# Eight of twelve fp32 recalls become three f32r products each, in an attention-with-memory plus gated feed-forward kernel

## The chip, the cores and the metric

The kernel runs on one core of a Trainium2 chip. The metric is the device time of one execution in microseconds (us); the time before is the median of three runs. Engines are TensorE (PE; PEld is its weight loading), VectorE (DVE), ScalarE (ACT), GpSimd (POOL) and SyncE (SP), which here only issues transfers. Each takes its own instructions in order and waits on semaphores for the others.

## The reference

A layer norm of x (2048 tokens of 448) feeds two branches whose results are added to x: attention with a memory over four blocks of 512 tokens and 16 heads of 28, and a gated feed-forward layer of width 1792. The part that matters, cut down:

```python
for s in range(N):                       # 4 blocks of 512 tokens
    ...
    p = softmax(logits, axis=-1)
    a_dot = jnp.einsum("bhqk,bhkd->bhqd", p, vs)
    pq = phi(qs)
    num = jnp.einsum("bhld,bhde->bhle", pq, M)
    den = jnp.einsum("bhld,bhd->bhl", pq, z)[..., None] + 1e-6
    o = g * (num / den) + (1.0 - g) * a_dot
    outs.append(o)
    M = M + jnp.einsum("bhld,bhle->bhde", phi(ks), vs)
    z = z + jnp.einsum("bhld->bhd", phi(ks))
```

A recall is `num` and `den` of four heads of one block: the memory M, with z as a further column, is multiplied by phi of the queries. Block 0 has an empty memory, so there are three blocks with four groups of heads each: twelve recalls.

## The kernel before

The work has a front, in which TensorE, ScalarE and VectorE follow the order of the program text, and a main part, in which the feed-forward products, the softmax attention and the output projection are interleaved. In the front GpSimd's and SyncE's queues are ordered by a scheduler when the program is built; they are not in the set `FRONT` of engines whose order is the text's.

The front goes block by block (L504, `b` from 0 to 3; "block 2" is the pass with `b` = 2). A pass first makes the values of its four token tiles: `values(b, t)` (L343) multiplies eleven pairs of high and low parts into one PSUM bank, and `store_values` (L338) copies the bank out on ScalarE. Large products throughout are made this way: a float32 operand is split into a high part of type f32r (a copy on ScalarE) and the rest (a subtraction), and three products, high by high, high by low and low by high, are summed in PSUM.

Then come seven strips of keys and queries, `keys_queries(b, c)` (L350), eleven products over 512 columns each, followed by ScalarE and VectorE work on the bank. Strips with queries also store phi of the queries to `fd[b]` (L368). The memory's update (L379) follows the strips; `mst` has two sets of four tiles of 112 x 128 (four heads of 28 rows), written in turn by even and odd blocks.

Recalls lag by one block: pass `b` = 2 recalls block 1 and pass 3 recalls block 2, four each; block 3's own four are made at the end of pass 3. In passes 2 and 3, `phi_queries` (L392) loads four phi tiles of 112 x 512 from DRAM, in buffers of the tag "e". The recall of group t - 1 stands behind `values(b, t)` for t = 1, 2, 3; the fourth stands behind the first `keys_queries`. `recall` (L397) is one fp32 product, which the profile shows as two passes of TensorE, into a bank of tag "m" or "pd"; then on VectorE a transpose (L402), `weigh` (an addition L132, a reciprocal L133, a weighting L136) and a second transpose (L404); then a transfer to `od` (L405) that GpSimd issues. In pass 2, VectorE also makes the statistics of the next block's rows, and ScalarE their root (L301), behind the first `values`.

Two shared sets of buffers are used by the change: tag "4k" (four buffers, L149; `qk` of `keys_queries`, later `hh`) and tag "2k" (two, L152; early weights, later `sg`). A `qk` buffer is free again when its transfer to `qd` (L363) has landed.

Of the kernel before, what the change touches and what calls it, by code (L numbers as in the profile page):

```python
# [9 lines left out]
F32 = mybir.dt.float32  # L10
F32R = mybir.dt.float32r
AF = mybir.ActivationFunctionType
# [4 lines left out]
P = 128  # L17
# [11 lines left out]
GW = HG * DH  # L29
# [32 lines left out]
def kernel(  # L62
# [11 lines left out]
    V, A, G, T = nc.vector, nc.scalar, nc.gpsimd, nc.tensor  # L74
# [33 lines left out]
    def x_block(b):  # L108
        return x[b * L:(b + 1) * L, :].rearrange("(t p) d -> p t d", p=P)
# [5 lines left out]
    def bank(name, tag):  # L115
        return ps.tile([P, L], F32, name=name, tag=tag, bufs=banks[tag])
# [10 lines left out]
    def weigh(pool, num, g, add):  # L127

        r = pool.tile([P, 16], F32, name="rc", bufs=2)
        n3 = num.rearrange("p (m c) -> p m c", c=32)  # L130
        if add:
            V.tensor_scalar_add(r, n3[:, :, DH], add)  # L132
            V.reciprocal(r, r)  # L133
        else:
            V.reciprocal(r, n3[:, :, DH])
        V.scalar_tensor_tensor(n3[:, :, :DH], n3[:, :, :DH], g, r.unsqueeze(2).to_broadcast([P, 16, DH]),  # L136
                               op0=ALU.mult, op1=ALU.mult)
# [6 lines left out]
    mid = ctx.enter_context(tc.tile_pool(name="mid", bufs=3, reuse_waits="tile"))  # L144
# [4 lines left out]
    def four_k(dtype, name):  # L149
        return mid.tile([P, 2, L], dtype, name=name, tag="4k", bufs=4)  # L150
# [125 lines left out]
    with tc.tile_pool(name="front", bufs=2) as sb, tc.manual_schedule(engines=FRONT):  # L276
# [7 lines left out]
        mst = [[sb.tile([GW, P], F32, name=f"mst{n}_{i}", bufs=1) for i in range(NG)] for n in range(2)]  # L284
# [3 lines left out]
        def statistics(b, t0, steps):  # L288

            stats = sb.tile([P, steps, 6], F32, name=f"stats{steps}")  # L290
            mv = sb.tile([P, steps, 2], F32, name=f"mv{steps}")
            vh = sb.tile([P, steps], F32, name=f"vh{steps}")
            for t in range(steps):
                V.bn_stats(stats[:, t, :], acc[b][:, t0 + t, :])
                V.bn_aggr(mv[:, t, :], stats[:, t, :])
            V.tensor_scalar(vh, mv[:, :, 1], EPS, -0.5, op0=ALU.add, op1=ALU.mult)
            return mv, vh

        def root(vh):
            y = sb.tile([P, vh.shape[1]], F32, name=f"y{vh.shape[1]}")  # L300
            A.activation(y, vh, AF.Sqrt, scale=-2.0)  # L301
            return y

        def rstd(mv, vh, y):

            steps = vh.shape[1]
            tm = sb.tile([P, steps], F32, name=f"tm{steps}")
            V.reciprocal(y, y)
            if steps == 1:
                V.tensor_scalar(tm, y, y, vh, op0=ALU.mult, op1=ALU.mult)  # L310
                V.tensor_scalar(y, tm, 1.5, y, op0=ALU.add, op1=ALU.mult)
            else:
                V.tensor_mul(tm, y, y)
                V.tensor_mul(tm, tm, vh)
                V.scalar_tensor_tensor(y, tm, 1.5, y, op0=ALU.add, op1=ALU.mult)
            return [(mv[:, t, 0:1], y[:, t:t + 1]) for t in range(steps)]

        def normalise(b, t, mean, y):
            xn = sb.tile([P, 512], F32, name="xn")
            V.tensor_scalar(xn[:, :D].rearrange("p (m h c) -> p h m c", h=H, c=4),  # L320
                              acc[b][:, t, :].rearrange("p (h m c) -> p h m c", h=H, c=4), mean, y,
                              op0=ALU.subtract, op1=ALU.mult)
            if b == 0:
                A.activation(xn[:, D:], xn[:, 384:D], AF.Copy)
            else:
                G.tensor_copy(xn[:, D:], xn[:, 384:D])
            return xn

        def turn(b, t, xn):
            transpose_split(bank("pt", "s"), xn, xs[b], t)  # L330
# [12 lines left out]
        def values(b, t):  # L343
            pv = bank("pv", "p")
            value_terms(b, t, pv, EARLY[1] if b == 0 else TERMS)
            store_values(b, t, pv)
# [45 lines left out]
        def phi_queries(b, i):  # L392
            phi = sb.tile([GW, L], F32, name="phi", tag="e", bufs=5)
            nc.sync.dma_start(phi, fd[b][i * GW:(i + 1) * GW])
            return phi

        def recall(b, i, phi):  # L397
            ts = sb.tile([P, L], F32, name="ts", bufs=1)
            tb = sb.tile([P, L], F32, name="tb", bufs=2)
            n2 = bank("n2", ("m", "pd")[i % 2])  # L400
            T.matmul(n2, mst[b % 2][i], phi, start=True, stop=True)  # L401
            V.transpose(ts, n2)  # L402
            weigh(sb, ts, gate[:, i:i + 1], MEM_EPS)
            V.transpose(tb, ts)  # L404
            nc.gpsimd.dma_start(od[b][P * i:P * (i + 1)], tb)  # L405
# [28 lines left out]
        def split_qk(c):  # L434
            r = raw_qk[c].rearrange("p (c n) -> p c n", c=4)
            A.activation(wqk[c][:, 0:4, :], r, AF.Copy)
            G.tensor_sub(wqk[c][:, 4:8, :], r, wqk[c][:, 0:4, :].bitcast(F32))
# [66 lines left out]
        for b in range(NB):  # L504
            last = b == NB - 1
            phi, xn = {}, {}
            if b > 1:
                phi = {i: phi_queries(b - 1, i) for i in range(NG)}
            st = None
            for t in range(3 if b == 0 else 0, NT):  # L510
                values(b, t)
                if b > 1 and t > 0:
                    recall(b - 1, t - 1, phi[t - 1])
                if b == 0:
                    split_qk(t)
                if last:
                    continue
                if t == (3 if b == 0 else 0):
                    mv, vh = statistics(b + 1, 0, NT)
                if t == (3 if b == 0 else 0):  # L520
                    st = mv, vh, root(vh)
                if t == (3 if b == 0 else 2):
                    A.activation(one, ident[:, 0:1], AF.Exp)
            if st and b > 0:
                st = rstd(*st)
                for n in range(2):
                    xn[n] = normalise(b + 1, n, *st[n])
            e = {}
            for k, c in enumerate((3, 4, 5, 6, 0, 1, 2) if last else range(7)):
                e[c] = keys_queries(b, c)  # L530
                if b == 0 and c + 4 < 7:
                    split_qk(c + 4)
                if k == 0:
                    if b > 1:
                        recall(b - 1, NG - 1, phi[NG - 1])
                    if b == 0:
                        st = rstd(*st)
                    if b == 0:
                        A.activation(gate, gate, AF.Exp, scale=-1.0)
                        V.tensor_scalar_add(gate, gate, 1.0)  # L540
                        V.reciprocal(gate, gate)
                        V.tensor_scalar(gate_n, gate, -1.0, 1.0, op0=ALU.mult, op1=ALU.add)
                if (b, k) in ((0, 3), (1, 0)):
                    with tc.issue_after(stored[b, c]):
                        nc.sync.dma_start(acc[b + 2], x_block(b + 2))
                if (b, k) in ((2, 1), (3, 0)):
                    with tc.issue_after(stored[b, c]):
                        next(ffn)
                if last:
                    if k > 0:  # L550
                        next(ffn)
                    if 2 <= k < 6:
                        phi[k - 2] = phi_queries(b, k - 2)
                    if k > 4:
                        begin[k - 5]()
                        recall(b, k - 5, phi[k - 5])
                    continue
                if 2 <= k < 6:
                    key_rows(k - 2, e[k - 2])
                if 4 <= k:  # L560
                    update(b, k - 4)
                if k == 6:
                    update(b, 3)
                n = k - 1 if b == 0 else k + 1
                if 2 <= n < 6:
                    turn(b + 1, n - 2, xn[n - 2])
                if 0 <= n < 4 and n not in xn:
                    xn[n] = normalise(b + 1, n, *st[n])
                if b == 2 and k == 6:
                    next(ffn)  # L570
            if last:
                for i in range(2):
                    for _ in range(FILLS[i]):
                        next(ffn)
                    if i == 0:
                        begin[2]()
                    recall(b, i + 2, phi[i + 2])
# [256 lines left out]
```

## Time and profile before

| | us |
|---|---|
| median of 3 runs (lowest, highest) | 689.46 (689.41, 689.59) |
| the profiled execution | 689.46 |
| its span, first to last instruction | 687.7 |
| TensorE, 77.80 to 95.20 us (17.40) | 17.40 busy |
| VectorE, same stretch | 15.40 busy |
| ScalarE, same stretch | 7.06 busy |
| GpSimd, same stretch | 2.48 busy |

A row of instructions reads: line, engine, operation, written and read tiles, shapes and count, then the busy time of all, the mean of one in ns, and the idle time of the engine ahead of them. A row of the timeline reads: start, length, engine, line, operation. The chain of waits follows the program back from its last instruction, at each step to what ended the wait.

### The profile page before, as it was taken

How to read it: one execution, taken by the hardware profiler on the slowest of the kernel's cores; microseconds unless marked ns; L12 is line 12 of the kernel's file. 1: busy time of each engine (PE TensorE's matmuls, PEld its weight loads, DVE VectorE, ACT ScalarE, POOL GpSimd, SP SyncE). 2: the span in 40 equal slices, each digit the busy share in tenths (PEclk: the TensorE clock that was granted, in tenths of full speed). 3: DMA queues.
4: the chain of work that ended last, by engine and by line, in shares of the span. 5: the costliest groups of instructions: out<-in, count | busy, mean ns of one | idle time of the engine just before them, and what ended most of it. 6: DMA issues, size and time to landing. Idle time of an engine off the chain costs nothing.

```text
span 687.7 us, 10438 instructions
## 1 busy us (share of the span) xinstructions
PE 681.7 (99%) x3594; PEld 566.6 (82%) x3594; DVE 567.4 (83%) x994; ACT 342.6 (50%) x563; POOL 151.3 (22%) x349
## 2 busy tenths in 40 slices
PE   8999999999999999999999999999999999999997
PEld 7898888778878787787878878787787878878897
DVE  6765795767788988998898989989898899889863
ACT  4837555343554555543655446454653565446320
POOL 3500020101223222232332222322322322222000
PEclk9999999999999999999999999999999999999999
DMA  7446556696233323243223252314333332423342
GB/s 267 181 150 238 198 214 242 249 330 174 71 94 92 80 86 86 56 128 112 56 64 107 57 141 56 109 47 116 82 94 77 96 71 64 95 79 95 95 153 106
DMA packets 45796, 84.37 MB, mean 123 GB/s; under 512 B 6320, under 2 KB 20400, under 8 KB 45232
## 3 DMA queue, kind: packets, MB, share of 16 engines
q1 hardware_dynamic: 42736, 76.37, 35.8%
q0 software_dynamic: 3008, 7.34, 4.9%
q8 instruction: 28, 0.46, 0.3%
q14 instruction: 24, 0.20, 0.1%
HBM read 51.05 MB, written 32.64 MB: 122 GB/s over the span
## 4 chain that ended last, share of the span: by engine, by line
PE 70%; DVE 14%; issue 9%; POOL 4%; DMA 1%; ACT 1%; SPq 0%; POOLq 0%; ACTq 0%
PE pgu L247 26%; PE pd L173 13%; PE pp L355 10%; PE po L771 5%; PE pv L335 5%; PE st L612 3%; PE pa L687 3%; DVE mx L629 3%; DVE w L666 2%; POOL w L627 2%; DVE acc L174 2%; PE pmm L383 2%; PE n L401 2%; DVE hh L259 1%; DVE mx L633 1%
## 5 line engine op out<-in xcount | busy, mean ns | idle before, releaser
L247 PE MATMUL pgu<-xs,wgu 128*128 128x512 f32 x1232 | 304.1, 394 | 0.0
L247 PEld LDWEIGHTS pgu<-xs,wgu 128*128 128x128 f32 x1232 | 228.2, 188 | 47.4 <-issue 2.2
L173 PE MATMUL pd<-wdn,hh 128*128 128x448 f32 x672 | 156.0, 367 | 0.0
L627 POOL TENSOR_SCALAR_AFFINE_SELECT w<-w 128x256 f32<-128x256 f32 (+1 forms) x160 | 81.2, 509 | 236.4 <-ACT w L616 183.6
L173 PEld LDWEIGHTS pd<-wdn,hh 128*128 128x128 f32 x672 | 122.5, 188 | 12.3 <-issue 0.6
L667 ACT ACTIVATE w<-w 128x1024 f32<-128x1024 f32 (+1 forms) x96 | 87.3, 915 | 65.0 <-DVE w L666 64.2
L666 DVE TENSOR_TENSOR w<-w,mb 128x1024 f32<-128x1024 f32 (+1 forms) x96 | 98.9, 1045 | 0.1
L616 ACT ACTIVATE w<-st 128x512 f32<-128x512 f32 x128 | 74.9, 590 | 45.3 <-PE st L612 44.9
L629 DVE TRANSPOSE_TENSOR_REDUCE mx<-w 128x32 f32<-128x1024 f32 x64 | 79.0, 1235 | 17.0 <-POOL w L627 17.0
L355 PE MATMUL pp<-xs,wqk 128*128 128x512 f32 x308 | 77.7, 401 | 0.0
L174 DVE TENSOR_TENSOR acc<-pd,acc 128x448 f32<-128x448 f32 x112 | 67.1, 599 | 1.2 <-PE pd L173 1.1
L355 PEld LDWEIGHTS pp<-xs,wqk 128*128 128x128 f32 x308 | 56.8, 188 | 13.4 <-issue 2.4
L258 ACT ACTIVATE hh<-sg 128x512 fp32r<-128x512 f32 x56 | 35.2, 628 | 56.4 <-DVE sg L256 49.3
L612 PE MATMUL st<-qk 84*128 84x128 f32 (+3 forms) x256 | 61.9, 312 | 0.0
L255 ACT ACTIVATE sg<-pgu 128x512 f32<-128x512 f32 x56 | 33.2, 594 | 49.4 <-PE pgu L247 49.2
L612 PEld LDWEIGHTS st<-qk 84*128 84x128 f32 x256 | 47.6, 189 | 6.9 <-ACT w L616 0.3
L656 DVE STREAM_TRANSPOSE mb<-top 128x1024 f32<-128x1024 f32 x32 | 39.8, 1242 | 10.5 <-POOL top L653 10.1
L362 DVE TENSOR_TENSOR qk<-pp,qk 128x512 fp32r<-128x512 f32 x28 | 19.3, 688 | 29.8 <-ACT e L360 23.7
L259 DVE SCALAR_TENSOR_TENSOR hh<-sg,hh 128x512 fp32r<-128x512 f32 x56 | 38.7, 691 | 2.6 <-ACT hh L258 2.4
L335 PE MATMUL pv<-wv,xs 128*128 128x448 f32 x176 | 39.6, 376 | 0.4 <-DVE xs L102 0.3
L687 PE MATMUL pa<-w,vv 128*32 128x128 f32 (+3 forms) x512 | 39.7, 436 | 0.2
L256 DVE SCALAR_TENSOR_TENSOR sg<-sg,pgu 128x512 f32<-128x512 f32 x56 | 37.3, 665 | 1.8 <-PE pgu L247 1.6
(100 smaller groups left out, 640.6 us busy)
## 6 DMA issues: line engine op xcount, KB each, us to landing
qk<-qd SPq DMA_DIRECT2D x192, 112.0 KB
qd<-qk SPq DMA_DIRECT2D x28, 512.0 KB
raw<-in_w_ffn SPq DMA_DIRECT2D x14, 512.0 KB
vd<-vst SPq DMA_DIRECT2D x4, 1024.0 KB
vv<-vd SPq DMA_DIRECT2D x16, 256.0 KB
od<-w POOLq DMA_DIRECT2D x16, 256.0 KB, 3.8
sums<-od SPq DMA_DIRECT2D x32, 128.0 KB
out<-acc SPq DMA_DIRECT2D x16, 224.0 KB
```

The source lines that it names most:

```text
L173: T.matmul(pd[:, :D], l, r, start=n == 0, stop=n == len(mms) - 1)
L174: V.tensor_add(acc[b][:, t, :], pd[:, :D], acc[b][:, t, :])
L247: T.matmul(dst, wgu[f][:, w, side * P:(side + 1) * P], xs[b][:, a, :], start=n == 0, stop=n == len(TERMS) - 1)
L335: T.matmul(pv[:, :D], xs[b][:, a, t * P:(t + 1) * P], wv[w], start=n == 0, stop=n == len(TERMS) - 1)
L355: T.matmul(pp, wqk[c][:, w, :], xs[b][:, a, :], start=n == 0, stop=n == len(TERMS) - 1)
L612: T.matmul(st[:, at:at + L - kb * P], self.qk[:KS, 1, h, kb * P:(kb + 1) * P], self.qk[:KS, 0, h, kb * P:], start=True, stop=True)
L616: A.activation(w, st, AF.Copy)
L627: G.affine_select(d, d, pattern=pattern, base=0, channel_multiplier=-1, compare_op=ALU.is_ge, fill=MASK)
L629: V.tensor_reduce(mx[:, 16 * (n - 1):16 * (n + 1)], w3[:, n // 2, :2 * L].rearrange("p (b n) -> p b n", n=32), axis=mybir.AxisListType.X, ...
L666: V.tensor_sub(w, w, m)
L667: A.activation(w, w, AF.Exp, scale=SCALE)
L687: T.matmul(pa[32 * j:32 * j + 32, kb * P:], self.vv[:, kb, 32 * j:32 * j + 32], self.pairs[j // 2].block(j % 2, kb), start=kb == 0, stop=k ...
```

## The change

Passes 2 and 3 call a new function `parts` behind each `values`, after the recall that stands there. It makes the high and low parts of a phi tile in a buffer of tag "4k" and those of the memory's tile in one of tag "2k", two copies on ScalarE and two subtractions on GpSimd, and returns three pairs of operands. `recall` then multiplies the three pairs into its bank. The four recalls of block 3 pass a plain tile and stay one fp32 product.

```diff
+        def parts(b, i, phi):
+
+            f = four_k(F32R, "phis")[:GW]
+            m = mid.tile([P, 4, P], F32R, name="ms", tag="2k", bufs=2)[:GW]
+            A.activation(f[:, 0, :], phi, AF.Copy)
+            G.tensor_sub(f[:, 1, :], phi, f[:, 0, :].bitcast(F32))
+            A.activation(m[:, 0, :], mst[b % 2][i], AF.Copy)
+            G.tensor_sub(m[:, 1, :], mst[b % 2][i], m[:, 0, :].bitcast(F32))
+            return [(m[:, a, :], f[:, w, :]) for a, w in ((0, 0), (0, 1), (1, 0))]
+
         def recall(b, i, phi):
...
             n2 = bank("n2", ("m", "pd")[i % 2])
-            T.matmul(n2, mst[b % 2][i], phi, start=True, stop=True)
+            terms = phi if isinstance(phi, list) else [(mst[b % 2][i], phi)]
+            for n, (l, r) in enumerate(terms):
+                T.matmul(n2, l, r, start=n == 0, stop=n == len(terms) - 1)
...
                 values(b, t)
-                if b > 1 and t > 0:
-                    recall(b - 1, t - 1, phi[t - 1])
+                if b > 1:
+                    if t > 0:
+                        recall(b - 1, t - 1, phi[t - 1])
+                    phi[t] = parts(b - 1, t, phi[t])
```

## The prediction

> **What bounds the kernel now.** I read the page's head first, then the chain of waits in order of time over the two stretches that the change touches.
>
> ```profile
> span 687.7 us, 10438 instructions
> PE 681.7 (99%) x3594; PEld 566.6 (82%) x3594; DVE 567.4 (83%) x994; ACT 342.6 (50%) x563; POOL 151.3 (22%) x349
> ```
>
> ```profile
> 78.06 4.42 PE pv L335 x22
> 82.48 0.86 PE n L401 x2
> 83.34 2.21 PE pv L335 x11
> 85.55 0.86 PE n L401 x2
> 86.41 2.21 PE pv L335 x11
> 88.61 0.86 PE n L401 x2
> 89.47 2.51 PE pp L355 x11
> 91.99 0.86 PE n L401 x2
> ...
> 115.00 4.42 PE pv L335 x22
> 119.42 0.86 PE n L401 x2
> ...
> 128.93 0.86 PE n L401 x2
> ```
>
> Columns: start, length, what (us). Each piece starts where the last one ended: in both stretches TensorE sets the time and waits for nothing. A recall is two passes, 0.86 us; the eleven products of `values` take 2.21, those of `keys_queries` 2.51. So what shortens a recall shortens the run, and what makes TensorE wait here lengthens it. The profiled run took 689.46 us, the median of the runs: span 687.7, 1.76 around it.
>
> **The change part by part.**
>
> *The products.* Three products over 512 columns, at the pace of the `keys_queries` group (2.51 / 11 = 0.228), take 0.685 in place of 0.86: 0.175 saved each, 1.4 us over eight, if nothing waits.
>
> *The splitting.* `parts(t)` puts two copies on ScalarE behind the store of `values(t)` and two subtractions on GpSimd. The nearest rows:
>
> ```profile
> L436 ACT ACTIVATE wqk<-stage 128x512 fp32r<-128x512 f32 x4 | 2.4, 621 | 0.0
> L377 ACT ACTIVATE kn<-pk 128x256 f32<-128x256 f32 x3 | 1.1, 370 | 0.0
> L324 ACT ACTIVATE xn<-xn 128x64 f32<-128x64 f32 x4 | 1.0, 254 | 3.8 <-DVE xn L320 3.8
> L437 POOL TENSOR_TENSOR wqk<-stage,wqk 128x512 fp32r<-128x512 f32 x4 | 5.1, 1293 | 4.8 <-ACT wqk L436 4.8
> L432 POOL TENSOR_TENSOR wv<-wv_raw,wv 128x448 fp32r<-128x448 f32 x4 | 4.6, 1167 | 5.9 <-ACT wv L431 5.9
> L326 POOL COPY xn<-xn 128x64 f32<-128x64 f32 x12 | 3.1, 262 | 38.3 <-DVE xn L320 24.6 <-PE pt L95 13.6
> L355 PE MATMUL pp<-xs,wqk 128*128 128x512 f32 x308 | 77.7, 401 | 0.0
> L355 PEld LDWEIGHTS pp<-xs,wqk 128*128 128x128 f32 x308 | 56.8, 188 | 13.4 <-issue 2.4
> ```
>
> The phi copy is L436's: 0.62. The memory's (128 columns) lies between 0.25 and 0.37; I take 0.29, and it ends under the first subtraction. Phi's subtraction is L437's: 1.29. The memory's subtraction has no row: between 0.26 (the 64-column copy) and 1.17 (448 columns); the line through L432 and L437, 1.97 ns a column, gives 0.54, which I take. Only the last recall's operands differ in partitions (112 for 128); I take no gain for that. The third product needs the memory's low part, so it comes last.
>
> *When the parts are ready, block 2.* The timeline of before:
>
> ```profile
> 80.31 0.55 ACT L339 ACTIVATE vst<-pv 128x448 f32<-128x448 f32 x1 [2.21 <-PE pv L335]
> 83.16 0.53 ACT L339 ACTIVATE vst<-pv 128x448 f32<-128x448 f32 x1
> 83.38 0.72 DVE L402 STREAM_TRANSPOSE ts<-n 128x512 f32<-128x512 f32 x1 [0.36 <-PE n L401]
> 84.63 0.68 DVE L136 SCALAR_TENSOR_TENSOR ts<-ts,gate,rc 128x448 f32<-128x448 f32 x1
> 86.38 0.76 POOL L405 DMA_DIRECT2D od<-tb  x1 [20.41 <-DVE tb L404]
> 89.44 0.56 POOL L405 DMA_DIRECT2D od<-tb  x1 [2.31 <-DVE tb L404]
> ...
> 117.25 0.55 ACT L339 ACTIVATE vst<-pv 128x448 f32<-128x448 f32 x1 [1.26 <-PE pv L335]
> ```
>
> Values 0 end at 78.06 + 2.21 = 80.27. ScalarE stores to 80.86 and copies to 81.48; GpSimd subtracts to 82.79 and 83.33 (an estimated 0.02 to start). TensorE is there at 82.48 and would want the third operand at 82.94. It waits, then loads weights (0.19) and multiplies (0.40), with 0.05 to wake (ScalarE took 0.04 from 80.27): recall 0 ends at 83.97, not 83.34: **+0.63**. Behind the waiting product stand values 2 and all that follows on TensorE.
>
> Recall 1: values 2 end at 86.18. ScalarE's store (83.16, held by the statistics as before) ends at 83.69, the copy at 84.31, the subtractions at 85.62 and 86.16: in time. It ends at 86.87, +0.46 against before. Recall 2: GpSimd also issues the store of recall 0, 3.00 us after `ts` starts (83.38 to 86.38), now at 87.01, until 87.77. Phi's copy is done at 87.39, so the store goes first and the subtractions end at 89.06 and 89.60. Values 3 end at 89.08; the third product waits and ends at 90.24 against 89.47: +0.77. If the subtractions go ahead of the store, it is 89.77, 0.47 less. Recall 3 has the 2.51 of `keys_queries` before it, so its parts (92.28) are in time: +0.59, or +0.12 with the other order. **Block 2 costs 0.59.**
>
> *Block 3* has no statistics; the store of values 0 stands at 117.25 here too, 0.04 after they end. So recall 0 ends at 120.91 against 120.28, +0.63. Recall 1 is in time, +0.46. Recall 2: store of recall 0 at 123.95 to 124.49, subtractions to 126.32, values 3 at 126.02: a wait of 0.25, +0.55. Recall 3 +0.37. **Block 3 costs 0.37.**
>
> *What else hides.* Phi must be in SBUF when ScalarE copies it, earlier than TensorE wanted it:
>
> ```profile
> 75.51 0.46 SPq L394 DMA_DIRECT2D phi<-fd  x1
> 78.19 0.33 SPq L363 DMA_DIRECT2D qd<-qk  x1
> ...
> 79.26 3.27 SPq L394 DMA_DIRECT2D phi<-fd  x3
> ```
>
> ```profile
> od<-tb POOLq DMA_DIRECT2D x3, 256.0 KB, 3.0
> ```
>
> By the landing time of a store of like size (3.0), the four are there by 78.5, 82.3 and, the last two, 85.5 at the latest; copies start at 80.86, 83.69, 86.77 and 89.7. If that cover is gone, the lateness goes to the recall one for one. No DMA is added. The new tiles share buffers with the `qk` stores, the last issued at 78.19, 11 us before the fourth part, and with `sg`, which comes after all eight. The chain starts before each phase of the remaining kernel, so nothing returns the 0.96.
>
> Sum: 0.59 + 0.37 = 0.96 on the profiled 689.46: **690.4 us**. With the subtractions ahead of the store and 0.26 for the small one, only the first recall of each block waits (0.28 less), and the sum is -0.35: 689.1. With 1.17, the first and third recalls' waits grow by 0.63 and, through the store issue, once more: 2.0 and 1.6 at the blocks' ends where 0.59 and 0.37 stood, about 693.0.
>
> **The rivals.**
>
> *The lock, slower.* Two inputs from SBUF on VectorE and a subtraction on GpSimd seem to exclude each other here:
>
> ```profile
> 25.55 1.30 POOL L437 TENSOR_TENSOR wqk<-wqk_raw,wqk 128x512 fp32r<-128x512 f32 x1 [2.81 <-ACT wqk L436]
> 25.80 1.08 DVE L313 TENSOR_TENSOR tm<-y 128x4 f32<-128x4 f32 x1
> 26.91 0.16 DVE L314 TENSOR_TENSOR tm<-tm,vh 128x4 f32<-128x4 f32 x1
> ```
>
> A four-column operation took 1.08 and ended with GpSimd's; its sister took 0.16. In the recall, L136 (0.68, two tiles) wants to start 1.25 after `ts` does (83.38 to 84.63), at 85.26, during a subtraction. If GpSimd's large and small subtraction go back to back it costs nothing; from the point where L136 slips in between, the small one is 0.69 late: block 2's recall 1 then waits to 87.49, recall 2 to 90.98, 0.74 more, and recall 2 of block 3 to 127.65, 0.69 more. 691.8 us. The Trainium skill ("SBUF — State Buffer", "Who interferes with whom") states this: whichever of the two starts first holds a shared port for its whole instruction, the other blocks. The row agrees that VectorE blocked; that GpSimd would then block behind L136 no row of these blocks shows.
>
> *A store issue ahead of a subtraction, slower.* GpSimd takes its queue in order. If the store of recall 0 stood ahead of recall 1's small subtraction, that one would end at 87.77 + 0.54 = 88.31 and recall 1 at 88.95, 2.1 late; later recalls take back 0.5. Two blocks: 3.2 more, 693.6. In program order, ahead of both subtractions every time, each of six recalls would wait about 3 us for the previous one's transposes, store issue and subtractions: +18, 708 us. Against it:
>
> ```profile
> 0.95 0.20 POOL L496 MEMSET heads<- 128x128 f32 x1
> ...
> 1.42 0.31 POOL L427 MEMSET vst<- 128x256 f32 x1
> ```
>
> L496 is written after L427, yet ran before: GpSimd's order follows what is ready, and the subtractions of recall 1 are ready at 84.31, 2.7 before the store. TensorE's clock never fell in the run of before:
>
> ```profile
> core 0: 687.7 us, clock 0.999
> ```
>
> The Trainium skill ("TensorE: Matmul & The Clock Gate", Part 1) says that it halves after some 3.4 us without work; waits of 3 us lie at that edge, and by that page the 708 would be some 5 to 10 us more, an estimate that no run here shows.
>
> *The whole gain, faster.* If no product waits: 689.46 - 1.4 = 688.06. Even 0.26 for the small subtraction leaves the first recall 0.1 late (83.05 against 82.94), so all GpSimd work would have to be quicker than its rows.
>
> *The change doesn't do what it says.* With 112 rows and new weights each time, three products might take 0.86 like the two passes (0.287 each). Then the 1.4 is lost beside the waits, some of which shrink: about 691.3.
>
> **How the numbers follow.** A measurement of this kernel tells about 0.2% (1.4 us) from no change: bounds 688.1 and 690.8. Forecast 0.55 (its own range 689.1 to 690.9, a tenth of it above 690.8), lock 0.17, store ahead 0.08 and program order 0.04, whole gain 0.10 (half below 688.1), no gain 0.06. Slower: 0.06 + 0.17 + 0.08 + 0.04 + 0.06 = 0.41. Faster: 0.05, and 0.03 for a reordered rest of the kernel. Same: 0.51. The range runs from the whole gain, 688.0, past the lock and the dear small subtraction to 693.0; store ahead, program order and half of what lies below are left out.
>
> **What would show it.** Right: recall groups of three products; the first of blocks 2 and 3 some 1.4 to 1.5 us long on the chain with a wait put down to GpSimd's subtraction of the memory; the second and fourth about 0.69. The blocks end 0.6 and about 1 us late on TensorE. Wrong: products far from 0.228, GpSimd's subtractions away from 1.29 and 0.54, VectorE's L136 well over 0.69 beside them, or an `od` issue between the two subtractions of one recall.

## The result, and the profile after

The changed kernel takes 695.37 us (median of 5 runs, 694.86 to 696.47) against 689.46 before: the ratio is 1.0089, with a 95% interval of 1.0078 to 1.0101. It is 5.9 us slower. The forecast was 690.4 with a range up to 693.0, so even the range missed it. The profiled run took the median, 695.37, with a span of 693.6 against 687.7.

The head of the page of the changed kernel: span, then for each engine busy time, share and instructions.

```profile
span 693.6 us, 10502 instructions
...
PE 683.1 (98%) x3602; PEld 567.1 (82%) x3602; DVE 573.4 (83%) x994; ACT 348.3 (50%) x579; POOL 165.7 (24%) x365
```

TensorE's busy time hardly moved (681.7 before), though eight more of its instructions stand there. VectorE has the same 994 instructions and is busy 6.0 us longer: something holds it. Where TensorE lost its time is in the chain of waits of the changed kernel, the same stretch that the prediction shows of the kernel before (start, length, what):

```profile
81.44 1.29 POOL phis L402
...
82.78 0.92 PE n L413 x2
...
83.73 0.73 DVE ts L414
...
84.48 1.30 DVE rc L132
...
86.09 0.69 DVE ts L136
...
86.81 0.72 DVE tb L416
...
87.83 0.06 POOL od L417
...
88.60 0.49 POOL ms L404
...
89.13 0.50 PE n L413
...
98.27 0.85 PE pt L95 x4
...
118.36 4.43 PE pv L335 x22
...
131.90 1.31 POOL phis L402
...
133.25 0.90 PE n L413 x2
134.15 2.06 PE pp L355 x9
```

Lines have moved: the recall's product is now L413, its transposes L414 and L416, its store L417, the subtractions L402 (phi) and L404 (memory). Recall 0 of block 2 ends at 83.70, 0.36 later than before (83.34). Then the chain leaves TensorE altogether. It runs through the whole back half of recall 0 on VectorE (transpose, L132, L136, transpose), through GpSimd's issue of that recall's store, and only then through GpSimd's small subtraction for recall 1. Recall 1 ends at 89.63 instead of 86.41, **3.22 us late**. Its own inputs had nothing to do with recall 0.

The timeline of the changed kernel at that place (start, length, engine, line, operation, idle time before it) shows both halves of it:

```profile
84.44 1.30 POOL L402 TENSOR_TENSOR phis<-phi,phis 112x512 fp32r<-112x512 f32 x1 [1.30 <-ACT phis L401]
84.48 1.29 DVE L132 TENSOR_SCALAR rc<-ts 128x16 f32<-128x16 f32 x1
...
87.83 0.75 POOL L417 DMA_DIRECT2D od<-tb  x1 [2.10 <-DVE tb L416]
88.60 0.48 POOL L404 TENSOR_TENSOR ms<-mst,ms 112x128 fp32r<-112x128 f32 x1
...
89.13 0.50 PE L413 MATMUL n<-phis,ms 112*128 112x512 f32 x1 [2.75 <-POOL ms L404]
```

First, GpSimd's order: phi's subtraction of recall 1 (84.44), **store of recall 0 (87.83), memory's subtraction of recall 1 (88.60)**. GpSimd has nothing to do from 85.74 to 87.83, but the store at the head of its queue waits for VectorE, and the small subtraction waits behind it. Second, VectorE's addition L132, sixteen elements of one input, takes 1.29 us where it takes 0.17 to 0.18 in the kernel before, and ends as GpSimd's subtraction does. It puts the store 1.1 us later still.

The groups of instructions of the changed kernel from 78 to 136 us (both blocks; busy time, mean ns, idle time ahead and its cause):

```profile
L402 POOL TENSOR_TENSOR phis<-phi,phis 112x512 fp32r<-112x512 f32 x8 | 10.4, 1297 | 31.2 <-ACT phis L401 31.1
L413 PE MATMUL n<-phis,ms 112*128 112x512 f32 x24 | 8.8, 434 | 3.2 <-POOL ms L404 2.7 <-POOL phis L402 0.3
L132 DVE TENSOR_SCALAR rc<-ts 128x16 f32<-128x16 f32 x7 | 6.8, 977 | 0.2
...
L404 POOL TENSOR_TENSOR ms<-mst,ms 112x128 fp32r<-112x128 f32 x8 | 3.7, 464 | 0.0
```

L132's mean is 977 ns. The subtractions themselves cost what was forecast, 1297 and 464 ns.

Followed by its landmarks on the chain, the loss of 5.9 us comes in three portions. Block 3's first values start at 118.36 instead of 115.00: **3.36 in block 2**. Most of it is recall 1; 0.41 come later in the block, at the transposes of block 3's normalised rows (L95, 0.85 where the kernel before takes 0.44), whose last piece GpSimd copies (L326, until 98.93) once VectorE has made it (L320). Block 3's recalls end at 134.15 instead of 129.79: **1.00 more in block 3**. A later landmark, the first full group of 32 attention products (`pa`, L701), starts at 209.11 instead of 203.19, and the offset stays the same from there on: **1.56 between the two**, outside the changed code.

### The profile page after: what moved, and what is told of

It reads as the page before. It is cut to its first block, busy times and chain, and to the rows that moved or that the text cites. A ratio compares the mean times of both kernels' runs of the same rounds, so it can differ in the third digit from the quotient of the medians.

```text
span 693.6 us, 10502 instructions
## 1 busy us (share of the span) xinstructions
PE 683.1 (98%) x3602; PEld 567.1 (82%) x3602; DVE 573.4 (83%) x994; ACT 348.3 (50%) x579; POOL 165.7 (24%) x365
## 4 chain that ended last, share of the span: by engine, by line
PE 67%; DVE 15%; issue 10%; POOL 5%; DMA 1%; ACT 1%; POOLq 0%; SPq 0%; ACTq 0%; DVEq 0%
PE pgu L247 25%; PE pd L173 13%; PE pp L355 9%; PE po L785 5%; PE pa L701 4%; PE st L626 3%; PE pv L335 3%; DVE mx L643 2%; POOL w L641 2%; DVE w L680 2%; PE pmm L383 2%; DVE acc L174 1%; DVE hh L259 1%; DVE mx L647 1%; DMA raw<-in_w_ffn 1%
## 5 line engine op out<-in xcount | busy, mean ns | idle before, releaser
L355 PE MATMUL pp<-xs,wqk 128*128 128x512 f32 x308 | 76.2, 396 | 0.0
L701 PE MATMUL pa<-w,vv 128*32 128x128 f32 (+3 forms) x512 | 39.7, 436 | 0.1
L335 PE MATMUL pv<-wv,xs 128*128 128x448 f32 x176 | 38.0, 367 | 0.4 <-POOL wv L444 0.2
```

The lines of the kernel that those rows point to most:

```text
L335: T.matmul(pv[:, :D], xs[b][:, a, t * P:(t + 1) * P], wv[w], start=n == 0, stop=n == len(TERMS) - 1)
L355: T.matmul(pp, wqk[c][:, w, :], xs[b][:, a, :], start=n == 0, stop=n == len(TERMS) - 1)
L701: T.matmul(pa[32 * j:32 * j + 32, kb * P:], self.vv[:, kb, 32 * j:32 * j + 32], self.pairs[j // 2].block(j % 2, kb), start=kb == 0, stop=k ...
```

## The experiments

The theory drawn from this profile had two parts. (a) The store stands ahead of the small subtraction on GpSimd in block 2. (b) GpSimd's subtraction holds VectorE's L132, which makes every store late, and the next subtractions stand behind the store. The main rival was that the lock alone, or GpSimd's load alone, is the cause. Every ratio is to the kernel before, run on the same chip. Three kernels, called "no addition", leave out the addition of 1e-6 in all twelve recalls.

### The store behind the small subtraction

```diff
-                    if t > 0:
-                        recall(b - 1, t - 1, phi[t - 1])
-                    phi[t] = parts(b - 1, t, phi[t])
+                    phi[t] = parts(b - 1, t, phi[t])
+                    if t > 0:
+                        recall(b - 1, t - 1, phi[t - 1])
```

In the recalls of both blocks, the only instruction on GpSimd whose place changes is the store of recall 0 in block 2.

> The one difference from the changed kernel: in block 2 GpSimd's issue of recall 0's store stands behind the small subtraction of recall 1 instead of ahead of it. Theory (the store's place in GpSimd's queue is the 3.2 us of block 2): recall 1 of block 2 ends near 86.8 us instead of 89.6, the third recall then waits for the store issue that stands ahead of its subtractions and gives back about 1 us, so the block gains 1.5 to 2 us; block 3 is as before; 691.9 to 693.9 us, the lower end if the late weight load after block 3 goes too. Rival (the subtractions are late because VectorE and GpSimd lock each other, wherever the store stands): recall 1 still ends after 88.5 us and the time stays at 695 us.

Measured: 693.96 us (692.80 to 694.43), ratio 1.0060 [1.0048, 1.0072]. The timeline of this kernel in block 2:

```profile
84.38 1.30 POOL L402 TENSOR_TENSOR phis<-phi,phis 112x512 fp32r<-112x512 f32 x1 [1.30 <-ACT phis L401]
84.43 1.29 DVE L132 TENSOR_SCALAR rc<-ts 128x16 f32<-128x16 f32 x1
85.64 0.46 POOL L404 TENSOR_TENSOR ms<-mst,ms 112x128 fp32r<-112x128 f32 x1
85.69 0.96 PE L413 MATMUL n<-phis,ms 112*128 112x512 f32 x3
...
87.78 0.75 POOL L417 DMA_DIRECT2D od<-tb  x1 [1.69 <-DVE tb L416]
88.32 1.56 DVE L132 TENSOR_SCALAR rc<-ts 128x16 f32<-128x16 f32 x1
88.55 1.29 POOL L402 TENSOR_TENSOR phis<-phi,phis 112x512 fp32r<-112x512 f32 x1
...
89.89 0.90 PE L413 MATMUL n<-phis,ms 112*128 112x512 f32 x2 [0.79 <-POOL phis L402]
```

Recall 1 now ends at 86.65, in time, where it ended at 89.63: the store's place costs recall 1 its 3 us, and (a) is shown. But the total comes down by only 1.4. Phi's subtraction of recall 2 stands behind the late store (87.78) and starts at 88.55; where no store is ahead of it, it starts at 87.17 (the kernel with the stores on SyncE, below). So TensorE waits at recall 2, and at recall 3 in the same way. Block 3's values start at 117.45: 2.45 of the 3.36 are still there. The stores are as late as before, because L132 is held as before (1.29, 1.56). The chain of this kernel runs, in block 2, through VectorE alone: three held additions, then the normalised rows of block 3 (L320, until 97.33), for which TensorE's transposes (L95, 97.37) wait. TensorE's own products end at 97.32, so both roads are equally late there.

### No addition, in the program's own order, and with the store behind

```diff
-            weigh(sb, ts, gate[:, i:i + 1], MEM_EPS)
+            weigh(sb, ts, gate[:, i:i + 1], 0.0)
```

L132 is gone; the reciprocal (now L135) reads the sums directly.

> The changed kernel, with the addition of 1e-6 ahead of the recalls' reciprocal left out; GpSimd's queue is in the same order. Theory (the addition, a VectorE operation of 0.18 us, was held 1.1 us by GpSimd's subtraction, and the store that GpSimd must issue before its next subtraction was late by that): recall 1 of block 2 ends 1.0 to 1.5 us earlier than in the changed kernel, at 88.1 to 88.6 us, and recall 3 of block 3 waits at most 0.2 us; 692.8 to 694.3 us. Rival (the reciprocal or the weighting is held in the addition's place): recall 1 ends after 89.0 us and the time stays within 0.5 us of 695.4. Second rival (the place of the store alone, at the price first worked out): 693.6 us with no change from the addition.

Measured: 693.53 (692.27 to 693.64), ratio 1.0054 [1.0041, 1.0067]. Its timeline in block 2:

```profile
84.39 1.30 POOL L402 TENSOR_TENSOR phis<-phi,phis 112x512 fp32r<-112x512 f32 x1 [1.30 <-DMA phi<-fd]
84.44 0.26 DVE L135 RECIPROCAL rc<-ts 128x16 f32<-128x16 f32 x1
84.73 1.44 DVE L136 SCALAR_TENSOR_TENSOR ts<-ts,gate,rc 128x448 f32<-128x448 f32 x1
...
87.23 0.75 POOL L417 DMA_DIRECT2D od<-tb  x1 [1.54 <-DVE tb L416]
```

The lock moves to the next instruction: the reciprocal passes beside the subtraction in its 0.26, and the weighting takes 1.44 in place of 0.69. The store comes 0.60 earlier (87.23 for 87.83) and recall 1 ends 0.60 earlier, at 89.03. So the store's time does follow from the lock. That another instruction is held in the addition's place, and that recall 1 ends after 89.0, was the rival's forecast; its time (695) was not met.

Both edits together:

> Both at once: GpSimd's store of recall 0 behind the small subtraction of recall 1, and the addition of 1e-6 left out of the recalls. Theory (the place of the store and the holding of VectorE together make all but the first recalls' waits, which are worth some 0.4 us a block): recall 1 of block 2 ends near 86.7 us, block 3 starts 0.5 to 1.5 us late against the kernel before, block 3 adds less than 0.6, nothing is lost after it; 690.0 to 691.3 us. Rival (a third cause in the changed kernel that neither edit touches): 692 us or more, and the chain names it.

Measured: 690.74 us (690.63 to 691.44), ratio 1.0020 [1.0011, 1.0028]. Over the median before, the loss is 5.9 as changed, 4.5 with the store moved, 4.1 without the addition, and 1.3 with both. By these medians neither edit alone takes away much more than a quarter, both together more than three quarters. How much each is worth by itself can't be read from this exactly: the profiled run without the addition also paid some 1.6 us to a slower TensorE clock (its `values` behind the wait took 3.79 in place of 2.21), of which more below. The one of its four runs whose mean clock was 1.000 took 692.27, a loss of 2.8, about half of the 5.9. With both edits, the profiled run (691.44, the slowest of eleven) starts block 3's values 1.35 late (116.35), of which 0.28 was there ahead of block 2 (78.34 for 78.06).

### GpSimd without stores

```diff
-            nc.gpsimd.dma_start(od[b][P * i:P * (i + 1)], tb)
+            nc.sync.dma_start(od[b][P * i:P * (i + 1)], tb)
```

Made once in the changed kernel and once, as a control, in the kernel before.

> The changed kernel with the recalls' stores issued by SyncE, so nothing on GpSimd waits for a recall. Theory: only the first recall of each block still waits (about 0.4 us late at its end), every later one takes 0.69 us instead of 0.86, and blocks 2 and 3 end within 0.3 us of the kernel before; 688.8 to 690.2 us. VectorE's addition behind a subtraction may still take 1.3 us, and costs nothing. Rival (GpSimd's subtractions are too slow by themselves or by the lock): other recalls wait too, 691.5 us or more. Second rival (SyncE's queue is now held by the stores): TensorE waits for transfers, 692 us or more.

> Control: the kernel before with the recalls' stores issued by SyncE. Theory: GpSimd has nothing to wait for in this stretch anyway and TensorE never stands still, 689.2 to 689.8 us, the same as before. Rival (SyncE's queue is held by the stores): slower by more than 1 us.

Measured: 702.31, ratio 1.0183 [1.0170, 1.0196], and the control 701.08, ratio 1.0169 [1.0156, 1.0182]. Both theories were wrong on the time, and the rival with SyncE's queue was right. As a way out this fails, and the control says that it has nothing to do with the change: SyncE's queue is held by the stores, and transfers for the attention come late (the control's chain has a piece of 3.49 us on the transfer `qk` from `qd`, at 168.20). But the front of the changed kernel is what the experiment was for. From its chain:

```profile
82.85 0.92 PE n L413 x2
...
85.99 0.78 PE n L413 x3
...
92.23 0.69 PE n L413 x3
...
119.81 0.92 PE n L413 x2
...
129.11 0.69 PE n L413 x3
129.80 2.51 PE pp L355 x11
```

Only the first recall of each block waits; the other six take 0.69 to 0.78, and block 3 ends at 129.80 against 129.79 before. In this very run L132 was held for 1.27 beside the subtraction of 84.51. The later additions met less of a subtraction here (0.47 and 0.40 in block 2). So in this run, beyond the first recall of a block, neither the lock nor GpSimd's load of some 14 us costs TensorE anything: here it is the stores in GpSimd's queue that hand VectorE's lateness on to TensorE. They are not the only road, as the kernels with a lead show below.

### One block alone

```diff
-                    phi[t] = parts(b - 1, t, phi[t])
+                    if b == 2:
+                        phi[t] = parts(b - 1, t, phi[t])
```

> The three products in the pass of block 2 alone; block 3's recalls are fp32 as before. Theory (block 2 costs 3.3 us, and the 1.5 us after block 3 come because block 3's stores are issued late into a stretch in which the DMA engines are full): block 3 starts 3.3 us late and passes it on unchanged; 692.5 to 693.1 us. Rival (the loss after block 3 follows from any delay of the front): 694.0 to 694.6 us.

> The three products in the pass of block 3 alone. Theory (in block 3 VectorE is held, so its strips go out late relative to TensorE, SyncE's queue and with it the next weights come late, and TensorE loses 1.0 to 1.5 us after the block although nothing was late before it): block 3 ends 0.8 to 1.1 us late, the second weights of the feed-forward part are split 24.5 to 25.3 us behind its first product instead of 21.8, and the loss grows to 1.9 to 2.6 us; 691.4 to 692.1 us. Rival (the loss after block 3 came from the whole delay of the front): it stays at 0.8 to 1.1 us, 690.3 to 690.6 us.

Measured, block 2 alone: 693.88 (692.89 to 695.33), ratio 1.0065 [1.0052, 1.0078]. Block 3 alone (`b == 3`): 690.75 (690.34 to 691.89), ratio 1.0022 [1.0012, 1.0033]. The excesses, 4.4 and 1.3, add up to 5.7 of the 5.9, but that is chance. The 4.4 holds a price of the clock (below) that the profiled run of the changed kernel did not pay; the one run of block 2 alone with a mean clock of 1.000 took 692.89, a loss of 3.4, as its theory had it. And 1.56 of the 5.9 are lost behind block 3, where neither block alone loses anything. For block 3 alone the theory's time was too high: it had this kernel carry the loss behind block 3 too, and the profiled run loses 1.0 in block 3 and nothing more.

The profiled run of block 2 alone holds a surprise. Its stretches (us, busy time and instructions of each engine, granted clock, DMA share, GB/s):

```profile
88.00:90.00 2.00, 0.75 (x2) 0.65 (x3) 0.00 (x0) 0.82 (x2) 1.99 (x3) 0.67 0.34 131
90.00:92.00 2.00, 2.00 (x7) 1.78 (x6) 1.81 (x4) 0.00 (x0) 0.83 (x2) 0.50 0.03 8
92.00:94.00 2.00, 2.00 (x7) 1.74 (x7) 0.73 (x2) 0.00 (x0) 0.57 (x1) 0.50 0.00 0
```

After a wait of 2.76 us at recall 1, TensorE's granted clock is 0.50 from 90 to 94: the eleven products of `values` take 4.11 instead of 2.21, the next recall 1.28 instead of 0.69. These 2.5 us are a price of the wait that the changed kernel's profiled run did not pay: its wait was 2.75 and its clock stayed at 1.00.

### A lead of one group

The parts of group 0 are made before the first `values`, those of group t + 1 behind `values(t)`, ahead of recall t - 1.

```diff
+                phi[0] = parts(b - 1, 0, phi[0])
...
                 if b > 1:
+                    if t < 3:
+                        phi[t + 1] = parts(b - 1, t + 1, phi[t + 1])
                     if t > 0:
                         recall(b - 1, t - 1, phi[t - 1])
-                    phi[t] = parts(b - 1, t, phi[t])
```

> The changed kernel with each splitting traced one step earlier: group 0 ahead of the first values, group t+1 behind values t. Theory (the waits are lateness of the parts): all eight recalls take 0.69 us without a wait, the gain of 1.4 us is whole, 688.0 to 688.9 us. Rival (the lock holds GpSimd or VectorE so long that parts or recalls come late all the same): waits on GpSimd's lines remain, 690 us or more.

Measured: 690.88 (690.70 to 693.80), ratio 1.0028 [1.0017, 1.0039]. In block 3 all four recalls take about 0.70 and the block gains 0.60. Block 2 still loses 2.12, against a theory that had no wait left. The timeline of this kernel, and below it the waits of its TensorE from 75 to 135 us (us in all, times, longest), show why:

```profile
79.39 1.30 POOL L402 TENSOR_TENSOR phis<-phi,phis 112x512 fp32r<-112x512 f32 x1 [13.48 <-ACT phis L401]
79.53 1.32 DVE L390 TENSOR_TENSOR mst<-mst,dm 112x128 f32<-112x128 f32 x1
...
87.98 3.20 DVE L132 TENSOR_SCALAR rc<-ts 128x16 f32<-128x16 f32 x1
...
88.21 1.29 POOL L402 TENSOR_TENSOR phis<-phi,phis 112x512 fp32r<-112x512 f32 x1
...
89.85 1.30 POOL L402 TENSOR_TENSOR phis<-phi,phis 112x512 fp32r<-112x512 f32 x1
```

```profile
PE n L413 <- POOL phis L402: 1.1, 1, 1.1
PE pt L95 <- DVE xn L320: 0.9, 1, 0.9
```

The first early subtraction holds the memory's update L390 (1.32 for 0.29), and L132 is held across three subtractions, 3.20 us, until the third of them ends at 91.15. VectorE has little room in block 2 (15.40 of 17.40 us before), and what it loses there is not made up. TensorE gets this lateness twice: at recall 2, whose subtraction again stands behind a late store, and at the transposes L95, which wait for VectorE's rows of block 3 with no store between. So the lock can reach TensorE without GpSimd's queue.

With the lead and no addition:

> Look-ahead by one step, and the addition of 1e-6 left out of the recalls. Theory (in block 2 the look-ahead lost 2.1 us because VectorE's addition was held up to 3.2 us by GpSimd's subtractions): block 2 loses less than 0.8 us, block 3 gains 0.6 us as before; 688.2 to 689.8 us. Rival (another VectorE operation is held instead, the update of the memory or the reciprocal): block 2 still loses 1.5 us or more, 690.4 to 691.2 us.

Measured: 690.12 (689.83 to 691.29), ratio 1.0011 [1.0003, 1.0020], between the theory's range and the rival's. The weighting L136 takes the lock over, 3.36 us at 88.05, and block 2 loses 1.13 in the profiled run (691.17, one of the slowest).

With the lead and the addition on ScalarE in the eight changed recalls (reading the sums, `A.activation(r, n3[:, :, DH], AF.Copy, bias=add)`):

> Look-ahead by one step, with the addition of 1e-6 made on ScalarE in the eight recalls, so the output is whole. Theory: as without the addition, plus two hand-overs of some 0.1 us in VectorE's chain; 688.3 to 690.0 us. Rival (ScalarE, which takes its queue in order, now waits for the transpose and stores and splits late): recalls wait on GpSimd again, 691 us or more.

Measured: 691.67 (690.22 to 693.74), ratio 1.0033 [1.0022, 1.0043]: no better than the lead alone, and outside the theory's range. No recall waits for GpSimd in its profiled run, so the rival's reason was not met either; TensorE waits 0.73 at L95 for VectorE's rows, and more is lost behind block 3 (below).

With the lead, in block 3 alone, where VectorE has room; block 2 keeps its fp32 recalls:

> Three products and the look-ahead in the pass of block 3 alone, where VectorE has room; block 2 is as in the kernel before. Theory: block 3 gains 0.6 to 0.7 us and nothing is lost after it as in the kernel with look-ahead in both blocks; 688.8 to 689.1 us, faster than the kernel before by a little under 0.1%. Rival (VectorE is held here too and the weights come late): 689.5 us or more.

Measured: 688.75 median of 12 runs (688.54 to 693.47) against 689.46; the ratio, which follows the mean of the runs (689.5), is 1.0001 [0.9989, 1.0012]. Its chain in block 3:

```profile
119.35 0.69 PE n L413 x3
...
128.40 0.69 PE n L413 x3
```

The two between take 0.69 and 0.71. No product waits, and the block ends 0.70 earlier, 0.07 of which it had at its start (114.93 for 115.00): nearly four times 0.17, as the prediction priced a product that finds its operands. Seven of the twelve runs are at 688.5 to 688.8, the whole gain; the others are at 689.1 to 693.5, and the profiled one (689.57) gives the gain back behind block 3. With an interval on both sides of 1, this version isn't shown to be faster than the kernel before, and none of the others comes near it.

### What is lost behind block 3

Where it can be followed, it goes mostly through the second feed-forward weight that is split on ScalarE (L85). In the changed kernel the chain has, behind block 3:

```profile
154.94 6.69 DMA raw<-in_w_ffn
...
161.71 1.07 ACT wgu L85
...
173.16 0.50 PE st L626
```

In the kernel before, TensorE never waits there. How late that split is, counted from the first gate-and-up product (`pgu`), in the profiled runs, beside the time lost behind block 3 (the two kernels with the stores on SyncE, which wait for other transfers there, are left out):

```
kernel                     split, us after   lost behind block 3, us
before                     21.75             -
block 2 alone              21.88             0
block 3 alone              22.93             0
store behind, no addition  23.03             0.4
no addition                23.35             0
lead, no addition          23.54             1.3
lead                       23.55             0
lead, block 3 alone        24.60             1.0
store behind               24.79             1.1
lead, addition on ScalarE  24.94             1.3
as changed                 25.21             1.6
```

Up to 23.55 nothing is lost this way; from 24.60 on it is about 1 us and more. (The 0.4 and the 1.3 of two kernels without the addition have another path: their chains go through a transfer of `od`, 5.88 and 6.32 us long.) The chain passes this split as changed, with the store behind and with the addition on ScalarE; with the lead in block 3 alone TensorE waits 0.69 for a ScalarE instruction (L633), and the chain does not go back to the split. So the table is a correlation, and the cause is argued. Part of the lateness is on SyncE's queue, which issues these transfers in turn. The waits of that queue (us in all, times, longest) in the changed kernel from 120 to 165 us:

```profile
SPq L394 <- DMA fd<-e: 7.5, 3, 3.0
```

and in the kernel before, from 120 to 162 us:

```profile
SPq L394 <- DMA fd<-e: 3.1, 3, 1.7
```

The loads of block 3's own phi wait longer for the stores of that phi to land, and the weight is issued behind them. Why these transfers take longer when the queues start a few us shifted to one another stays open: no run changed that alone.

## Why the prediction was wrong

**The step that failed** is recall 1 of block 2: "ScalarE's store [...] ends at 83.69, the copy at 84.31, the subtractions at 85.62 and 86.16: in time. It ends at 86.87, +0.46 against before." It ended 3.22 late. The phi subtraction did end at 85.74; the memory's ended at 89.08, since the store of recall 0 stood ahead of it. The prediction had this case among its rivals (693.6, chance 0.08) and argued it down: "GpSimd's order follows what is ready, and the subtractions of recall 1 are ready at 84.31, 2.7 before the store". That order is fixed when the program is built. Two memsets, which wait for nothing, said that the order isn't the text's; they could not say how the scheduler ranks a store against a subtraction. An `od` issue between the two subtractions of one recall was among the prediction's own signs of being wrong. The rival's price was 2.1 at recall 1 of both blocks; it came in block 2 alone, at 3.22, because the store was also held up by the second step. Moving the text of `parts` by one statement moved the store behind the subtraction.

**The second step** is the lock: the prediction looked at L136 alone, as the instruction with two tiles. In its sum the lock costs nothing; as a rival it stood at 691.8, with a chance of 0.17, by GpSimd waiting behind L136. It was the one-input L132 that was held, 1.29 us for 0.18. The Trainium skill ("SBUF — State Buffer", "Who interferes with whom") counts `tensor_scalar` among the operations that can enter a mode with two ports, where their operands meet its conditions, and so contend with GpSimd, which the prediction passed over. The durations agree with contention; which mode the instruction was in, no run here shows. What follows from it is not a slower VectorE as such: the store is 1.1 later, and everything behind the store on GpSimd with it; and in block 2 the normalised rows come later too. No run took the subtractions off GpSimd.

**Terms that held.** Three products take 0.69 (forecast 0.685). Phi's copy and subtraction take 0.62 and 1.29, as forecast; the memory's subtraction 0.45 to 0.48 (0.54 was taken, between 0.26 and 1.17). The first recall of each block does wait for its parts, 0.36 and 0.37 late rather than 0.63, mostly because the small subtraction was quicker and started beside the end of the large one. With no stores on GpSimd, the front ends 0.01 us from where it did; the prediction's own steps give +0.12 a block where no store is ahead of a subtraction.

**Block 3** was forecast at +0.37 and lost 1.00. Here the order is the harmless one, both subtractions of recall 1 ahead of the store. Recall 2 waits about as forecast (0.41 late for 0.55), behind the store of recall 0 (127.33). Recall 3 was forecast in time and is not: recall 1's L132 is held for 1.37, its store comes at 131.32, and the subtractions for recall 3 stand behind it. This wait is in the chain: phi's subtraction at 131.90, the products at 133.25.

**"So nothing returns the 0.96"** said that the chain begins before each later phase. That covered only what could be gained back, not what more could be lost: 1.56 went behind block 3.

**The clock.** The rival with program order said that waits of 3 us lie at the edge of the 3.4 us that the Trainium skill gives ("TensorE: Matmul & The Clock Gate", Part 1). The runs put the edge lower: in one of them the clock halved after a wait of 2.2 us.

## What to carry to other kernels

When work is added to an engine that also issues transfers, write down its whole queue in its built order, and ask of each issue what it waits for: one store that waits for another engine makes everything behind it as late as that engine. A readiness argument doesn't give that order; a scheduler's tie must be counted as a real chance. And a subtraction on GpSimd of 1.3 us can cost VectorE as much, if it meets an instruction that it holds (here L132, L136 and L390); it is hidden only where VectorE has that much room.

## What the runs showed of the hardware

- A GpSimd subtraction of 1.29 us held VectorE's addition over sixteen elements (0.18 alone), the weighting with two tiles (0.69 alone, 1.44 held) and the memory's update (0.29 alone, 1.32 held), and did not hold a reciprocal (0.26) that ran beside it. Where GpSimd's subtractions came back to back, one VectorE instruction was held over two or three of them in some places (1.81 as changed, 3.20 and 3.36 with the lead) and came in between two of them in others (1.56 with the store behind). The reverse also occurs: without the addition, the memory's subtraction took 0.84 to 0.89 in places where it met a held weighting, instead of 0.46. That is the wait of GpSimd behind L136 that the prediction's rival had, at 0.4 in place of 0.69.
- TensorE's granted clock fell to 0.50 for 3.4 us (89.3 to 92.7) at a wait of 2.20 us (no addition) and for 6.8 us, twice as long (88.7 to 95.5), at one of 2.76 us (block 2 alone), and not at one of 2.75 us (the changed kernel). It fell 0.7 us after the first wait had ended, and 0.6 before the second did. The length of the wait alone doesn't decide it. It cost 2.5 us in the profiled run of block 2 alone. It is also why that kernel's times spread: 692.89 with a mean clock of 1.000, 693.8 to 695.3 with 0.995 to 0.997. The Trainium skill ("TensorE: Matmul & The Clock Gate", Part 1) describes a window of 3.4 us that runs freely, so that it matters where a wait falls in it; that one wait of 2.75 us passes and another doesn't agrees with this, and so do the 3.4 and 6.8 us; that a wait of 2.20 us is enough does not agree with a whole idle window.
